# Attention scores from zero-padded states, fewer split operands, and a planner that keeps GpSimd and VectorE apart

## The chip, the core and the metric

The program runs on one core of one Trainium2 chip. The metric is the device time of one execution in microseconds (us). TensorE is called PE here (PEld is its weight load, which overlaps the matmuls), VectorE is DVE, ScalarE is ACT, GpSimd is POOL, and SyncE (SP) issues every DMA of this kernel. TensorE has two clock levels, 1.2 and 2.4 GHz; the profile gives the granted share of the higher one (PEclk: 1.00 is 2.4 GHz).

## What is computed

The reference, cut to what matters. Batch 8, 8 heads, 512 positions, 32 states, head size 64; the two feed-forward layers have 4608 tokens, width 512 and inner width 1536.

```python
def _attn_ref(x, state):                      # x (8,8,512,64), state (8,8,32,64)
    scores = scale * x @ state^T              # softmax over the 32 states  -> xread = a @ state
    scores2 = scale * state @ x^T             # softmax over the 512 tokens -> sread = a2 @ x
    return concatenate([xread, sread], axis=2)

x = attention output as rows of 512           # 8 * (512 + 32) = 4608 tokens
x = ((x @ w_a) * (x @ w_b)) @ w_out           # first layer
x = (silu(x @ w_gate) * (x @ w_val)) @ w_out  # second layer
```

Only the last array is returned.

## The kernel before, in words

**Numbers.** Most products are computed as sums of products of split operands: `hi_lo` (lines 319 to 328) makes `hi`, a rounded copy that PE takes at one pass (`R32`), on ACT (line 324), and `lo = x - hi` on DVE or POOL (`subtract`, line 317). A product then takes three matmuls (hi·hi, hi·lo, lo·hi). A matmul on unsplit `F32` operands needs no preparation but costs PE more. Weights come as 64-bit floats; `convert` (lines 339 to 379) turns each into 32-bit ones with two ACT, three or so DVE and one POOL instruction, the last of which (line 375, an integer add) only POOL may do.

**Stages.** The batches are called blocks 0 to 7, and `s` is the block of all state rows. About the first 760 us compute attention and the first layer: attention block by block, the products of states and weights (`state_w`, lines 431 and 432), the first layer's two products (`gemm`, line 645) and its output product (`out_part`, line 680). In the shadow of that the second layer's weights are converted, combined and written back to DRAM (`second_weights`, line 700 on). From about 760 us on the second layer runs over four pairs of blocks: at the start of a pair `operands` forms sums of its inputs (line 738) and splits them, then `second` runs products pA to pD (line 750), combinations (764, 771) and output products (`unit`, line 844; partial sums at 862).

**Attention.** `attention` runs once a block and `quad` twice (a quad is two pairs of heads, j = 0 and 1, each of 64 score rows). `quad` loads two `xt` tiles, makes scores `sT` (128 rows, 512 tokens), and calls `softmax1` (lines 520 to 553: DVE transposes and reductions, result split for the first layer) and `softmax2` (lines 555 on: result `sread`). There are two ways through it, chosen by `split`, which is true for blocks from `FROM_SPLIT` = 2 on:

- unsplit (blocks 0, 1): for each j one F32 matmul of 64 weight columns into its own half of the PSUM rows (line 511), one copy to `sT`; in `softmax2` one copy of the turned weights `pa` to `a2`, and four F32 matmuls with `xn` (line 605).
- split (blocks 2 to 7): `xt` is split; the states' tile `stt` has hi in one half of its 128 columns and lo in the other (lines 471 to 474), so that two matmuls a j give both halves (line 494), which ACT copies across (line 500) and DVE adds (line 503); in `softmax2` `pa` is split into `a2`, `xn` (1024 columns) into `xnh` and `xnl`, and twelve matmuls follow.

**Order.** Nothing is issued as it is written. Every instruction is a task of `Program` with buffers, dependencies, a due time `by`, and for some a `start`; `order` is a list scheduler that plays the whole program through with the costs at lines 62 to 67 and gives each engine's queue an order. A task that ACT, DVE or POOL may do goes to the engine that comes free, unless another is planned to finish it earlier. At run time each engine takes its queue strictly in that order. All DMAs are on SP's queue. PSUM banks, and the shared buffer classes `w` (44) and `h` (20), are counted in the plan.

Of the kernel before, what the change touches and what calls it, by code (L numbers as in the profile page):

```python
# [44 lines left out]
FROM_SPLIT = 2  # L45
# [18 lines left out]
HOP_US, PE_HOP_US = 0.15, 0.3  # L64
DMA_US, DMA_ISSUE_US, DMA_BYTES_PER_US = 2.2, 0.5, 3.6e5

# [3 lines left out]
def act(n):  # L70
    return {"ACT": ACT_US[0] + ACT_US[1] * n}
# [11 lines left out]
class Buf:  # L83


    def __init__(self, tag, name, make, after=None):
        self.tag, self.name, self.make, self.after = tag, name, make, after
        self.t = None
        self.parts = {}
        self.tasks = set()  # L90
# [10 lines left out]


class Program:
# [8 lines left out]
    def add(self, engines, fn, r=(), w=(), by=1e9, start=0.0, size=0):  # L112
# [24 lines left out]
        self.tasks.append(t)  # L137
        return t

    def order(self):  # L140
# [16 lines left out]
        wire = 0.0  # L157
        events = []
# [9 lines left out]
        while events:  # L168
# [18 lines left out]
            for e, heap in ready.items():  # L187
                if free[e] > now + 1e-9:
                    continue
                held = []  # L190
                while heap:
# [21 lines left out]
                    free[e] = end = now + us  # L213
                    main = max(main, t.main)
# [27 lines left out]
class Kernel:  # L242
# [32 lines left out]
    def bank(self, name, out=None):  # L275

        if out is not None:
            return self.ring(f"po{out}", 1, name, self.ps)
        return Buf("pt", name, lambda: self.ps.tile([P, 512], F32, tag="pt", bufs=ROOM["pt"], name=name))
# [4 lines left out]
    def ring(self, tag, n, name, pool=None, dtype=F32, shape=(512,)):  # L284
# [6 lines left out]
        )  # L291
        old.append(b)
# [162 lines left out]
    def attention(self, b, start, span, split, by_x, by_s):  # L455


        nc, p = self.nc, self.p
        raw_st = self.load(
            self.h_buf(f"strt{b}"), self.st_t[b], P * 1024, lambda t: t[:, :256], start=start  # L460
        )
        st = lambda: raw_st.t[:, :256].rearrange("p (j n) -> p j n", n=64)
        tt = None
        if split:
            tt = self.w_buf(f"stt{b}", R32, (NPAIR, P))
            for par in range(2):
                o = 64 * par
                hi = lambda par=par, o=o: tt.t[:, par::2, o:o + 64]
                lo = lambda par=par, o=o: tt.t[:, par::2, 64 - o:128 - o]
                src = lambda par=par: st()[:, par::2]  # L470
                self.p.add(act(128), lambda e, hi=hi, src=src: nc.scalar.copy(hi(), src()), [raw_st], [(tt, (par, 0))])
                self.subtract(
                    lo, src, lambda hi=hi: hi().bitcast(F32), dve_pool(128), [raw_st, (tt, (par, 0))], [(tt, (par, 1))]
                )
        return [
            self.quad(b, g, start + span * g / 2, span, raw_st, st, tt, by_x, by_s) for g in range(2)
        ]

    def quad(self, b, g, t0, span, raw_st, st, tt, by_x, by_s):

        nc, p = self.nc, self.p
        split = tt is not None
# [3 lines left out]
        if split:  # L486
            tmp = self.h_buf(f"tmp{nm}")
            for j in range(2):
                s = self.split(f"xts{nm}_{j}", x[j])
                ps = self.bank(f"psc{nm}_{j}")  # L490

                def fn(pe, j=j, s=s, ps=ps):
# [3 lines left out]
                self.pe(2 * PASS_US, fn, [tt, s], [ps], by=t0 + span * 0.15)  # L496
                own, oth = slice(64 * j, 64 * j + 64), slice(64 - 64 * j, 128 - 64 * j)
                kw = {"by": t0 + span * 0.15 + 2}
                p.add(
                    act(512), lambda e, own=own, oth=oth, ps=ps: nc.scalar.copy(tmp.t[own], ps.t[oth]),  # L500
                    [ps], [(tmp, j)], **kw
                )
                self.vec(512, lambda v, own=own, ps=ps: v.tensor_tensor(
                    out=sT.t[own], in0=ps.t[own], in1=tmp.t[own], op=ALU.add
                ), [ps, (tmp, j)], [(sT, j)], **kw)
        else:
            ps = self.bank(f"psc{nm}", g if b == 0 else None)

            def fn(pe, ps=ps):
                for j in range(2):  # L510
                    pe.matmul(
                        ps.t[64 * j:64 * j + 64], lhsT=st()[:, 2 * g + j], rhs=x[j].t, start=True, stop=True
                    )

            self.pe(8 * PASS_US, fn, [raw_st, x[0], x[1]], [ps], by=t0 + span * 0.15)
            self.copy(lambda: sT.t, lambda ps=ps: ps.t, 512, [ps], [sT], by=t0 + span * 0.15 + 2)
        x_hl = self.softmax1(b, g, sT, by_x)
        self.softmax2(b, g, sT, split, by_s)
        return x_hl

    def softmax1(self, b, g, sT, by):
# [7 lines left out]
        self.vec(512, lambda v: v.transpose(sn.t, sT.t), [sT], [sn], **kw)  # L529
        self.vec(  # L530
            512, lambda v: v.tensor_reduce(mx.t[:, :, 0], grouped(sn.t), axis=AX.X, op=ALU.max), [sn], [mx], **kw
# [8 lines left out]
            512, lambda v: v.tensor_reduce(sm.t[:, :, 0], grouped(sn.t), axis=AX.X, op=ALU.add), [sn], [sm], **kw  # L540
# [11 lines left out]
        self.vec(512, lambda v: v.transpose(at.t, sn.t), [sn], [at], **kw)  # L552
        return self.split(f"xs{nm}", at, **kw)

    def softmax2(self, b, g, sT, split, by):
# [11 lines left out]
        self.vec(620, first, [sT], [st], start=by - 35, **kw)  # L567
# [17 lines left out]
        if split:  # L585
            a2 = self.split(f"a2{nm}", pa, psum=True, **kw)
            xh, xl = self.w_buf(f"xnh{nm}", R32, (1024,)), self.w_buf(f"xnl{nm}", R32, (1024,))
            self.hi_lo(xn, lambda: xn.t, xh, lambda: xh.t, xl, lambda: xl.t, 1024, **kw)
            parts = [xh, xl]
        else:  # L590
            a2 = self.h_buf(f"a2{nm}")
            self.copy(lambda: a2.t, lambda: pa.t, 512, [pa], [a2], **kw)
            parts = [xn]
        ps = self.bank(f"psr{nm}")

        def fn(pe):
            terms = []
            for c in range(4):
                l, r = slice(c * P, (c + 1) * P), slice(c * 256, (c + 1) * 256)
                if split:  # L600
                    terms += [(a2.t[:, ha, l], parts[hx].t[:, r]) for ha, hx in ((0, 0), (0, 1), (1, 0))]
                else:
                    terms.append((a2.t[:, l], xn.t[:, r]))
            for n, (l, r) in enumerate(terms):
                pe.matmul(ps.t[:, :256], lhsT=l, rhs=r, start=n == 0, stop=n == len(terms) - 1)

        self.pe(1.32 if split else 1.75, fn, [a2, *parts], [ps], **kw)
# [398 lines left out]
def laid_out(inputs):  # L1006
# [6 lines left out]
    st_t = np.zeros((B, 2, D, NPAIR, 2, NS), state.dtype)  # L1013
    for h in range(2):
        st_t[:, h, :, :, h] = sp[:, :, h].transpose(0, 3, 1, 2)
    arrays["st_t"] = st_t.reshape(B, P, NPAIR * 2 * NS)
# [32 lines left out]
```

## Time and profile before

| | us |
|---|---|
| median of 3 runs | 1563.6 (1561.76 to 1568.19) |
| the profiled execution | 1562.1 |
| its span, first to last instruction | 1560.3 |
| PE busy | 1482.2 (95%) |
| DVE busy | 1109.7 (71%) |
| ACT busy | 675.9 (43%) |
| POOL busy | 360.3 (23%) |
| mean granted clock of PE | 0.985 |

Matmuls overlap in the pipeline, so the busy time of PE is the time in which at least one is under way; what PE takes for a matmul is read from the start of one to the start of the next. An engine's busy time includes time in which an instruction is under way but held up.

### The profile page before, as it was taken

The numbers are of one execution on the slowest core, as the hardware profiler recorded it, in microseconds if no ns is written. First come the engines' busy times: TensorE is split into PE (matmuls) and PEld (weight loads), VectorE is DVE, ScalarE is ACT, GpSimd is POOL, SyncE is SP. The second block draws the span as 40 slices with busy tenths as digits, with TensorE's granted clock in tenths as the row PEclk, the third lists the DMA queues.
The fourth block names the chain that finished last, engine by engine and source line by source line (L and its number), as shares of the span: only waits on it lengthen the run. The fifth ranks groups of instructions, "written<-read, shape, count | busy, mean of one in ns | idle before, by whom it ended". The sixth has DMA issues, their size and how long they took to land.

```text
span 1560.3 us, 19362 instructions
## 1 busy us (share of the span) xinstructions
PE 1482.2 (95%) x6792; PEld 1218.3 (78%) x6792; DVE 1109.7 (71%) x1676; ACT 675.9 (43%) x1196; POOL 360.3 (23%) x256
## 2 busy tenths in 40 slices
PE   4798899899999999999999989999999999999998
PEld 1577687688887888898777778888788887888887
DVE  8999767866789898776686896555855568545554
ACT  6676655653556576554442432221413123222220
POOL 3525212421234343333321340000200021000000
PEclk9899999899999999999999999999999999999999
DMA  7665564563455555656875668646464555622411
GB/s 285 211 236 197 177 220 145 176 205 122 152 189 206 202 205 216 230 203 216 334 259 200 238 236 305 220 157 221 167 231 168 189 202 173 218 95 108 162 68 68
DMA packets 111185, 304.84 MB, mean 195 GB/s; under 512 B 11760, under 2 KB 13808, under 8 KB 111088
## 3 DMA queue, kind: packets, MB, share of 16 engines
q1 hardware_dynamic: 111088, 303.61, 54.8%
q8 instruction: 53, 0.87, 0.2%
q14 instruction: 44, 0.36, 0.1%
HBM read 222.30 MB, written 80.74 MB: 194 GB/s over the span
## 4 chain that ended last, share of the span: by engine, by line
PE 52%; DVE 8%; issue 2%; DMA 1%; ACT 1%; POOL 1%; SPq 0%; DVEq 0%; POOLq 0%; ACTq 0%
PE pu L844 15%; PE pC L750 7%; PE pB L750 7%; PE pA L750 7%; PE pD L750 3%; PE po L680 3%; PE p L645 3%; PE p_s L645 2%; DVE s L738 1%; PE pvs L645 1%; PE pgs L645 1%; PE pus L844 1%; DVE x L317 1%; PE po_s L680 1%; DVE t L764 1%
## 5 line engine op out<-in xcount | busy, mean ns | idle before, releaser
L680 PE MATMUL po<-hs,wo 128*128 128x512 f32 x1152 | 289.7, 395 | 2.6 <-ACT hs L324 1.5
L645 PE MATMUL p<-xs,swh 128*128 128x512 f32 x768 | 243.4, 398 | 15.0 <-ACT xs L324 5.5
L680 PEld LDWEIGHTS po<-hs,wo 128*128 128x128 f32 x1152 | 218.3, 191 | 48.6 <-ACT hs L324 1.9
L645 PEld LDWEIGHTS p<-xs,swh 128*128 128x128 f32 x768 | 144.7, 191 | 50.2 <-DVE a L664 6.5
L645 PE MATMUL p<-xs,swl 128*128 128x512 f32 x384 | 151.8, 395 | 1.2 <-DVE swl L317 1.1
L750 PE MATMUL pB<-x,w 128*128 128x512 f32 x576 | 146.6, 390 | 2.0 <-DVE t L764 2.0
L750 PE MATMUL pA<-x,wg 128*128 128x512 f32 x576 | 148.0, 393 | 0.0
L844 PE MATMUL pu<-wo,hv 128*128 128x512 f32 x576 | 140.6, 389 | 0.0
L844 PE MATMUL pu<-wo,hu 128*128 128x512 f32 x576 | 138.6, 389 | 0.0
L750 PEld LDWEIGHTS pB<-x,w 128*128 128x128 f32 x576 | 108.2, 188 | 25.4 <-DVE t L764 2.8
L750 PEld LDWEIGHTS pA<-x,wg 128*128 128x128 f32 x576 | 109.5, 190 | 23.1
L844 PEld LDWEIGHTS pu<-wo,hu 128*128 128x128 f32 x576 | 107.9, 188 | 22.2
L844 PEld LDWEIGHTS pu<-wo,hv 128*128 128x128 f32 x576 | 107.9, 188 | 22.2
L768 ACT ACTIVATE av<-t 128x512 f32<-128x512 f32 x48 | 30.4, 632 | 211.2 <-DVE t L764 211.1
L317 POOL TENSOR_TENSOR hv<-av,hv 128x512 fp32r<-128x512 f32 x21 | 33.8, 1610 | 379.9 <-ACT hv L324 346.6
L764 DVE TENSOR_TENSOR t<-c,pB 128x512 f32<-128x512 f32 x96 | 65.6, 683 | 72.0 <-PE pB L750 71.7
L317 POOL TENSOR_TENSOR hs<-a,hs 128x512 fp32r<-128x512 f32 x40 | 62.5, 1562 | 179.1 <-ACT hs L324 169.6
L664 DVE TENSOR_TENSOR a<-a,p 128x512 f32<-128x512 f32 x96 | 65.5, 682 | 50.4 <-PE p L645 48.5
L324 ACT CAST hs<-a 128x512 fp32r<-128x512 f32 x96 | 59.6, 621 | 69.3 <-DVE a L664 56.2
L645 PEld LDWEIGHTS p<-xs,swl 128*128 128x128 f32 x384 | 73.3, 191 | 17.6 <-DVE swl L317 2.0
L750 PE MATMUL pC<-x,wv 128*128 128x512 f32 x288 | 75.3, 398 | 9.9 <-DVE c L764 9.9
L862 DVE TENSOR_TENSOR part<-part,pu 128x512 f32<-128x512 f32 x64 | 43.8, 684 | 51.1 <-PE pu L844 51.1
(205 smaller groups left out, 2682.1 us busy)
## 6 DMA issues: line engine op xcount, KB each, us to landing
w<-w SPq DMA_DIRECT2D x120, 512.0 KB, 5.3
sw<-swo SPq DMA_DIRECT2D x96, 256.0 KB, 2.5
wg<-w2g SPq DMA_DIRECT2D x48, 512.0 KB, 4.7
wv<-w2v SPq DMA_DIRECT2D x48, 512.0 KB, 5.0
wo<-w2o SPq DMA_DIRECT2D x48, 512.0 KB, 5.6
swr<-sw SPq DMA_DIRECT2D x47, 512.0 KB, 5.1
raw_w<-in_wab SPq DMA_DIRECT2D x24, 512.0 KB, 6.5
xt<-in_xt SPq DMA_DIRECT2D x32, 256.0 KB, 5.5
```

The lines of the kernel that those rows point to most:

```text
L317: lambda e: self.by_engine[e].tensor_tensor(out=out(), in0=in0(), in1=in1(), op=ALU.subtract), r, w, **kw
L324: self.p.add(act(n), lambda e: self.nc.scalar.copy(hi(), src()), [src_buf], [hb], **kw)
L645: pe.matmul(ps.t[:, :n], lhsT=l, rhs=r, start=i == 0, stop=i == last)
L664: self.vec(n, lambda v, a=a, pb=pb: v.tensor_tensor(out=a.t[:, :n], in0=a.t[:, :n], in1=pb.t[:, :n], op=ALU.mult), [pb], [a])
L680: pe.matmul(ps.t[:, :n], lhsT=wo[f].t[:, hw, c], rhs=hs.t[:, hh, :n], start=st, stop=sp)
L738: self.vec(512, lambda e, o=o, a=a, b=b, op=op: e.tensor_tensor(out=o.t, in0=a.t, in1=b.t, op=op), [a, b], [o])
L750: pe.matmul(ps.t, lhsT=w.t[:, hw, c], rhs=x.t[:, hx], start=start and i == n == 0, stop=stop and i == 1 and n == 2, skip_group_check=True)
L764: self.vec(512, lambda e: e.tensor_tensor(out=out.t, in0=ta(), in1=tb(), op=op), [a, b], [out])
L768: p.add(act(n), lambda e: nc.scalar.activation(out=a.t[:, :n], in_=g.t[:, :n], func=AF.Sigmoid), [g], [a])
L844: pe.matmul(ps.t, lhsT=h.t[:, hh, c], rhs=wo[f].t[:, hw], start=f == steps[0] and i == 0, stop=f == steps[-1] and i == 2)
L862: self.vec(w, lambda v: v.tensor_tensor(out=to(), in0=part.t[:, j % 2, :w], in1=ps.t[:, :w], op=ALU.add), [ps, (part, j)], [ok], by=by)
```

## The change

`FROM_SPLIT` becomes 4: blocks 2 and 3 take the unsplit way for the scores. The states come zero-padded from the host: for each pair j the tile has 128 columns, of which the other j's 64 are zero, so all matmuls of a quad add into one PSUM bank of 128 rows. A split quad takes six matmuls (three terms for each j) and one copy; an unsplit one takes two full-width F32 matmuls. In `softmax2` nothing is split any more, in any block. The planner's part: a task that has no PSUM buffer is marked `port` (in `Program.add`), apart from DVE's transposes and reductions, which are marked not; a variable `shared` holds until when POOL or a port task of DVE is planned to run, and while it lies ahead POOL takes nothing and DVE takes only tasks without the mark. POOL takes a task that DVE could do too only while DVE has at least 0.9 us of unmarked work ready (`BESIDE_US`). The planned delay between engines, `HOP_US`, goes from 0.15 to 0.25.

```diff
-FROM_SPLIT = 2
+FROM_SPLIT = 4
-HOP_US, PE_HOP_US = 0.15, 0.3
+HOP_US, PE_HOP_US = 0.25, 0.3
+BESIDE_US = 0.9
@@ Program.add
+        t.port = not any(b.psum for b in t.bufs) if port is None else port
@@ Program.order
+        shared = 0.0
+                blocked = shared > now + 1e-9 and e in ("DVE", "POOL")
+                    if blocked and (e == "POOL" or t.port):
+                        held.append(item)
+                        continue
+                    if e == "POOL" and "DVE" in t.engines and sum(
+                        q[2].engines["DVE"] for q in ready["DVE"] if q[2].engine is None and not q[2].port
+                    ) < BESIDE_US:
+                        held.append(item)
+                        continue
+                    if e == "POOL" or e == "DVE" and t.port:
+                        shared = end
@@ attention
-        raw_st = self.load(
-            self.h_buf(f"strt{b}"), self.st_t[b], P * 1024, lambda t: t[:, :256], start=start
-        )
+        raw_st = self.load(self.h_buf(f"strt{b}"), self.st_t[b], start=start)
+        tt = self.split(f"stt{b}", raw_st) if split else None
@@ quad, split (before)
-                s = self.split(f"xts{nm}_{j}", x[j])
-                ps = self.bank(f"psc{nm}_{j}")
-                    for h in range(2):
-                        pe.matmul(ps.t, lhsT=tt.t[:, 2 * g + j], rhs=s.t[:, h], start=h == 0, stop=h == 1)
-                    act(512), lambda e, own=own, oth=oth, ps=ps: nc.scalar.copy(tmp.t[own], ps.t[oth]),
-                self.vec(512, lambda v, own=own, ps=ps: v.tensor_tensor(
-                    out=sT.t[own], in0=ps.t[own], in1=tmp.t[own], op=ALU.add
@@ quad, unsplit (before)
-                    pe.matmul(
-                        ps.t[64 * j:64 * j + 64], lhsT=st()[:, 2 * g + j], rhs=x[j].t, start=True, stop=True
-                    )
@@ quad (after)
+        if tt is not None:
+            xs = [self.split(f"xts{nm}_{j}", x[j]) for j in range(2)]
+            terms = lambda: [
+                (tt.t[:, hs, cols[j]], xs[j].t[:, hx]) for j in range(2) for hs, hx in ((0, 0), (0, 1), (1, 0))
+            ]
+        else:
+            xs = x
+            terms = lambda: [(raw_st.t[:, cols[j]], x[j].t) for j in range(2)]
+        def fn(pe):
+            pairs = terms()
+            for n, (l, r) in enumerate(pairs):
+                pe.matmul(ps.t, lhsT=l, rhs=r, start=n == 0, stop=n == len(pairs) - 1)
+        self.pe((8 if tt is None else 6) * PASS_US, fn, [tt or raw_st, *xs], [ps], by=t0 + span * 0.15)
+        self.copy(lambda: sT.t, lambda: ps.t, 512, [ps], [sT], by=t0 + span * 0.15 + 2)
@@ softmax2
-            a2 = self.split(f"a2{nm}", pa, psum=True, **kw)
-            self.hi_lo(xn, lambda: xn.t, xh, lambda: xh.t, xl, lambda: xl.t, 1024, **kw)
+        a2 = self.h_buf(f"a2{nm}")
+        self.copy(lambda: a2.t, lambda: pa.t, 512, [pa], [a2], **kw)
+                pe.matmul(ps.t[:, :256], lhsT=a2.t[:, l], rhs=xn.t[:, r], start=c == 0, stop=c == 3)
@@ laid_out
-    st_t = np.zeros((B, 2, D, NPAIR, 2, NS), state.dtype)
+    st_t = np.zeros((B, 2, D, NPAIR, 2, 2, NS), state.dtype)
```

The states' tile that is loaded for each block thus grows from 128 to 256 KB.

## Rows read from the trace of the kernel before

**Rows 1.** Busy us (and instructions) by stage: PE, PEld, DVE, ACT, POOL; clock, DMA.
```profile
0.00:60.00 60.00, 31.76 (x72) 15.16 (x72) 52.05 (x75) 38.29 (x64) 25.92 (x25) 0.97 0.72 260
60.00:200.00 140.00, 126.69 (x539) 100.58 (x538) 126.24 (x204) 102.65 (x191) 52.09 (x39) 0.97 0.60 209
200.00:310.00 110.00, 102.44 (x457) 82.01 (x456) 82.11 (x125) 61.92 (x110) 30.37 (x21) 0.95 0.50 169
310.00:700.00 390.00, 380.23 (x1920) 323.28 (x1921) 306.80 (x476) 225.24 (x403) 131.11 (x89) 0.99 0.55 193
700.00:950.00 250.00, 238.28 (x1023) 194.12 (x1022) 189.18 (x270) 102.42 (x174) 67.52 (x45) 0.97 0.69 253
950.00:1300.00 350.00, 347.20 (x1530) 286.57 (x1529) 215.22 (x315) 89.33 (x152) 37.24 (x23) 1.00 0.55 197
1300.00:1560.00 260.00, 255.56 (x1261) 216.60 (x1259) 138.05 (x216) 56.00 (x107) 16.07 (x15) 1.00 0.38 131
```

**Rows 2.** Waits of PE from 60 to 310 us: total, times, longest.
```profile
PE p L645 <- ACT xs L324: 5.5, 1, 5.5
PE sw L431 <- DVE a L311: 4.3, 1, 4.3
```

**Rows 3.** Waits of PE from 310 to 1000 us: total, times, longest.
```profile
PE pC L750 <- DVE c L764: 6.9, 3, 4.5
```

**Rows 4.** A DVE reduction: duration in ns, minimum, median, maximum.
```profile
L531 DVE TENSOR_REDUCE mx<-sn x16: 628/678/686, 9.2 to 610.8; 128x16 f32<-128x512 f32 x16
```

**Rows 5.** One of DVE's subtractions at L317, the same columns.
```profile
L317 DVE TENSOR_TENSOR xts<-xt,xts x16: 678/692/1785, 68.0 to 599.1; 128x512 fp32r<-128x512 f32 x16
```

**Rows 6.** Timeline of DVE around 560 us: start, us, instruction.
```profile
558.25 3.45 DVE L317 TENSOR_TENSOR xnl<-xn,xnh 128x1024 fp32r<-128x1024 f32 x2
561.62 1.78 DVE L317 TENSOR_TENSOR xts<-xt,xts 128x512 fp32r<-128x512 f32 x1
```

**Rows 7.** Timeline of POOL in the same stretch.
```profile
560.58 2.28 POOL L317 TENSOR_TENSOR xts<-xt,xts 128x512 fp32r<-128x512 f32 x1
```

**Rows 8.** DVE's operand sums at L738, durations as in rows 4.
```profile
L738 DVE TENSOR_TENSOR s<-s,x2l x8: 679/1479/1776, 748.7 to 1285.2; 128x512 f32<-128x512 f32 x8
```

**Rows 9.** Chain that ended last: start, us, what; two split quads, twelve passes.
```profile
571.79 2.87 PE psr L605 x24
576.50 2.72 PE p L645 x12
```

**Rows 10.** Timeline of PE: two unsplit quads of L605 and what follows.
```profile
136.45 3.72 PE L605 MATMUL psr<-xn,a 128*128 128x256 f32 x16 [0.65 <-ACT a L309]
139.82 0.58 PE L680 MATMUL po<-hs,wo 128*128 128x512 f32 x1
```

**Rows 11.** Timeline of PE: unsplit scores of two quads, then the first layer's first product.
```profile
13.63 2.55 PE L511 MATMUL psc<-xt,strt 128*64 128x512 f32 x4 [3.01 <-DMA xt<-in_xt]
...
40.05 1.98 PE L511 MATMUL psc<-xt,strt 128*64 128x512 f32 x4
41.96 1.22 PE L645 MATMUL p<-xs,swh 128*128 128x512 f32 x2
42.98 0.63 PE L645 MATMUL p<-xs,swl 128*128 128x512 f32 x1
```

**Rows 12.** Groups by shape: count, busy us, mean ns, idle before.
```profile
L503 DVE TENSOR_TENSOR sT<-psc,tmp 64x512 f32<-64x512 f32 x24 | 16.5, 687 | 1.5 <-ACT tmp L500 1.2
...
L317 DVE TENSOR_TENSOR xnl<-xn,xnh 128x1024 fp32r<-128x1024 f32 x11 | 15.9, 1448 | 0.7 <-ACT xnh L324 0.5
...
L500 ACT COPY tmp<-psc 64x512 f32<-64x512 f32 x24 | 14.0, 582 | 3.1 <-PE psc L494 2.5
...
L317 DVE TENSOR_TENSOR a<-pa,a 128x512 fp32r<-128x512 f32 x12 | 7.7, 682 | 2.4 <-ACT a L324 2.4
```

**Rows 13.** POOL's integer add of the conversions, durations as in rows 4.
```profile
L375 POOL TENSOR_TENSOR cv_w<-cv_w x24: 1282/1601/2274, 11.4 to 284.4; 128x512 int32<-128x512 int32 x24
```

**Rows 14.** Timeline of DVE in the start: one run of subtractions.
```profile
22.79 3.81 DVE L317 TENSOR_TENSOR w<-cv_w,w 64x512 fp32r<-64x512 f32 x5
```

More of the change, by code (lines that the diff above doesn't have):

```diff
@@ L88, in __init__ @@
         self.t = None
+        self.psum = False
         self.parts = {}
@@ L100, in __init__ @@
         self.engine, self.main = None, 0.0
+        self.port = False
 class Program:
@@ L110, in __init__, with add @@
         self.first = 0.0
-    def add(self, engines, fn, r=(), w=(), by=1e9, start=0.0, size=0):
+    def add(self, engines, fn, r=(), w=(), by=1e9, start=0.0, size=0, port=None):
         deps, bufs = set(), []
@@ L278, in bank @@
             return self.ring(f"po{out}", 1, name, self.ps)
-        return Buf("pt", name, lambda: self.ps.tile([P, 512], F32, tag="pt", bufs=ROOM["pt"], name=name))
+        b = Buf("pt", name, lambda: self.ps.tile([P, 512], F32, tag="pt", bufs=ROOM["pt"], name=name))
+        b.psum = True
+        return b
     def dram(self, name, shape, dtype=F32):
@@ L291, in ring @@
         )
+        b.psum = pool is self.ps
         old.append(b)
@@ L458, in attention, with quad @@
         nc, p = self.nc, self.p
-        raw_st = self.load(
-            self.h_buf(f"strt{b}"), self.st_t[b], P * 1024, lambda t: t[:, :256], start=start
-        )
[L462 to L473, printed above, removed]
-                )
+        raw_st = self.load(self.h_buf(f"strt{b}"), self.st_t[b], start=start)
+        tt = self.split(f"stt{b}", raw_st) if split else None
         return [
-            self.quad(b, g, start + span * g / 2, span, raw_st, st, tt, by_x, by_s) for g in range(2)
+            self.quad(b, g, start + span * g / 2, span, raw_st, tt, by_x, by_s) for g in range(2)
         ]
-    def quad(self, b, g, t0, span, raw_st, st, tt, by_x, by_s):
-        nc, p = self.nc, self.p
-        split = tt is not None
+    def quad(self, b, g, t0, span, raw_st, tt, by_x, by_s):
         nm = f"{b}_{g}"
@@ new lines, in quad @@
+        ps = self.bank(f"psc{nm}", g if b == 0 else None)
+        cols = [slice((2 * g + j) * P, (2 * g + j + 1) * P) for j in range(2)]
+        if tt is not None:
[3 more added lines that the diff above has]
+            ]
+        else:
+            xs = x
+            terms = lambda: [(raw_st.t[:, cols[j]], x[j].t) for j in range(2)]
@@ L517, in quad @@
+        def fn(pe):
[4 more added lines that the diff above has]
+        self.copy(lambda: sT.t, lambda: ps.t, 512, [ps], [sT], by=t0 + span * 0.15 + 2)
         x_hl = self.softmax1(b, g, sT, by_x)
-        self.softmax2(b, g, sT, split, by_s)
+        self.softmax2(b, g, sT, by_s)
@@ L528, in softmax1 @@
         kw = {"by": by}
-        self.vec(512, lambda v: v.transpose(sn.t, sT.t), [sT], [sn], **kw)
+        self.vec(512, lambda v: v.transpose(sn.t, sT.t), [sT], [sn], port=False, **kw)
         self.vec(
-            512, lambda v: v.tensor_reduce(mx.t[:, :, 0], grouped(sn.t), axis=AX.X, op=ALU.max), [sn], [mx], **kw
+            512, lambda v: v.tensor_reduce(mx.t[:, :, 0], grouped(sn.t), axis=AX.X, op=ALU.max), [sn], [mx], port=False, **kw
         )
@@ L539, in softmax1 @@
         self.vec(
-            512, lambda v: v.tensor_reduce(sm.t[:, :, 0], grouped(sn.t), axis=AX.X, op=ALU.add), [sn], [sm], **kw
+            512, lambda v: v.tensor_reduce(sm.t[:, :, 0], grouped(sn.t), axis=AX.X, op=ALU.add), [sn], [sm], port=False, **kw
         )
@@ L551, in softmax1, with softmax2 @@
         at = self.h_buf(f"at{nm}")
-        self.vec(512, lambda v: v.transpose(at.t, sn.t), [sn], [at], **kw)
+        self.vec(512, lambda v: v.transpose(at.t, sn.t), [sn], [at], port=False, **kw)
         return self.split(f"xs{nm}", at, **kw)
-    def softmax2(self, b, g, sT, split, by):
+    def softmax2(self, b, g, sT, by):
         nc = self.nc
@@ L565, in first @@
             v.tensor_scalar(out=st.t[:, 1:2], in0=st.t[:, 0:1], scalar1=-SCALE, scalar2=None, op0=ALU.mult)
-        self.vec(620, first, [sT], [st], start=by - 35, **kw)
+        self.vec(620, first, [sT], [st], start=by - 35, port=False, **kw)
         self.p.add(act(512), lambda e: nc.scalar.activation(
@@ L584, in softmax2 @@
         xn = self.load(self.w_buf(f"xn{nm}", F32, (1024,)), self.xn[b, g], P * 4096, start=by - 25)
-        if split:
-            a2 = self.split(f"a2{nm}", pa, psum=True, **kw)
-            xh, xl = self.w_buf(f"xnh{nm}", R32, (1024,)), self.w_buf(f"xnl{nm}", R32, (1024,))
-            self.hi_lo(xn, lambda: xn.t, xh, lambda: xh.t, xl, lambda: xl.t, 1024, **kw)
[L589 to L593, printed above, removed]
+        a2 = self.h_buf(f"a2{nm}")
+        self.copy(lambda: a2.t, lambda: pa.t, 512, [pa], [a2], **kw)
         ps = self.bank(f"psr{nm}")
         def fn(pe):
-            terms = []
             for c in range(4):
                 l, r = slice(c * P, (c + 1) * P), slice(c * 256, (c + 1) * 256)
[L600 to L607, printed above, removed]
+                pe.matmul(ps.t[:, :256], lhsT=a2.t[:, l], rhs=xn.t[:, r], start=c == 0, stop=c == 3)
+        self.pe(1.75, fn, [a2, xn], [ps], **kw)
         sr = self.h_buf(f"sr{nm}")
@@ L1012, in laid_out @@
     sp = state.reshape(B, NPAIR, 2, NS, D)
-    st_t = np.zeros((B, 2, D, NPAIR, 2, NS), state.dtype)
+    st_t = np.zeros((B, 2, D, NPAIR, 2, 2, NS), state.dtype)
     for h in range(2):
-        st_t[:, h, :, :, h] = sp[:, :, h].transpose(0, 3, 1, 2)
-    arrays["st_t"] = st_t.reshape(B, P, NPAIR * 2 * NS)
+        for j in range(2):
+            st_t[:, h, :, j::2, j, h] = sp[:, j::2, h].transpose(0, 3, 1, 2)
+    arrays["st_t"] = st_t.reshape(B, P, NPAIR * 4 * NS)
     st_1 = np.zeros((2, 2, D, H, NS, 4), state.dtype)
```

17 lines of the change are left out of this document (removed).

## The prediction

> **What bounds the kernel now.** I read the busy times by stage first, then what PE waited for, then the durations of DVE's and POOL's instructions against each other.
>
> The stages [rows 1] show that PE's stream sets the time nearly everywhere: from 950 to 1300 us PE is busy for 347.2 of 350 us. Time is lost where PE idles: 28.2 us before 60 us, 13.3 from 60 to 200, 7.6 from 200 to 310, 9.8 from 310 to 700, 11.7 from 700 to 950, 2.8 from 950 to 1300, and 4.4 at the end, where the last outputs drain. The granted clock falls in the same stages: one less the clock, times the length, is 4.2 us for 60 to 200, 5.5, 3.9 and 7.5 for the next three. So from 60 to 1300 us 45 us are idle and about 21 more were run at the lower clock level after an idle spell: 66 us is the most that a better order could return there.
>
> DVE is why PE idles. Idle share and DVE load go together [rows 1]: DVE 90% busy and PE idle 9.5% (60 to 200), 79% and 2.5% (310 to 700), 61% and 0.8% (950 to 1300). The waits name DVE's late results, or ACT's that follow them [rows 2, 3].
>
> Part of DVE's load is no work. A reduction, with one input, is 678 ns in the median and never over 686 [rows 4]; a subtraction, with two inputs in SBUF, is 692 in the median and reaches 1785 [rows 5]. Around 561 us both sides are to be seen: DVE's `xts` takes 1.78 us while POOL runs another for 2.28 us [rows 6, 7]. The two engines take turns at such operations, and the one that comes second is shown as busy. At the switch between pairs in the second layer half of one kind of sums are held up so (median 1479 against a minimum of 679 ns) [rows 8], and PE waits for their products.
>
> **The change part by part.**
>
> *PE: longer.* A 512-column pass is 2.72/12 = 0.227 us [rows 9]. Scores of a split quad go from four passes to six: 0.453 us, times 8 quads (blocks 4 to 7), 3.6 us. In `softmax2` two split quads took 2.87 us [rows 9], two unsplit 139.82 - 136.45 = 3.37 [rows 10]: 0.25 us a quad, times 12, 3.0 us. Blocks 2 and 3 replace four passes (0.91 us) by two full-width F32 matmuls of 512 columns. No row has one at full clock. From below: the F32 matmul of 256 columns is 3.37/8 = 0.42 us, so twice that for 512, 1.69 a quad. From above: the pair of half-width ones took 1.91 us at the lower clock level [rows 11] (that it was the lower one is seen from the two passes behind, 1.02 us), the two side by side; one after the other at full clock that is again 1.91. I take 1.69, which comes from full clock and full width: 0.78 times 4 quads, 3.1 us (4.0 at most). Sum: 9.7 us (10.6). All this lies in stages where PE is the bound and counts in full.
>
> Blocks 0 and 1 lose the side-by-side pair: 1.9 us more a quad at the lower level. Three of these four quads run by 16.2 us, where PE idles for its inputs anyway, but the fourth stands directly ahead of the first product at 41.96 us [rows 11]. Cost 1.9 us, between 0 (if it is ordered earlier) and 3.8 (if DVE's first input, too, is late by 1.9). The pair in one row, both done in 1.91 us, is the trace's side of this [rows 11]. The Trainium skill, "TensorEngine Tiling (Array Packing)", section Performance Considerations, has the rule, and it speaks against this part: weights of at most 64 columns can run as two column tiles at once. By it half-width matmuls would keep blocks 2 and 3 at 0.84 us a quad in place of 1.69, and the sum below would be 4 x 0.85 + 1.9 = 5.3 us lower; the padding gives that up, so the sum stays with the rows.
>
> *DVE and ACT: shorter.* Gone are the 24 half-height sums (687 ns, 16.5 us of DVE), the 24 copies across (14.0 us of ACT), 12 subtractions from PSUM (7.7 us of DVE) and the split of `xn` (11 subtractions of 1.22 to 1.45 us on DVE, one on POOL, and 12 casts on ACT) [rows 12]; 8 of the `xts` subtractions, 0.69 us in the median [rows 5]. Added are 12 copies of `sT` on ACT or DVE, 0.6 to 0.7 us each, and slightly longer splits of the states. DVE loses some 40 us, net of half the copies.
>
> *The planner: POOL's share.* POOL has 257 instructions [rows 1]; 72 are the integer adds of the conversions, which stay. Some 180 could go to DVE. A moved one costs DVE 0.69 us; one left on POOL holds up DVE's neighbour by up to 1.78 - 0.69 = 1.09 us [rows 5, 6]. So moving is about even for DVE's load, and I count it as 0. What is gained is order: a held-up instruction on DVE holds all that is queued behind it, PSUM copies for PE among them, and the plan now lets those pass first. In turn a marked task that is ready waits, in the plan, for POOL's instruction to end; behind it on its queue nothing stands, since the plan issues others first.
>
> *What comes back.* I read it from the relation between DVE load and PE idle above.
> - 60 to 200 us: 8 sums (5.5 us) and 8 `xts` (5.5 us) fall out, 2 copies come in: 126.2 becomes about 117 of 140, 83%. Between 79% (2.5%) and 90% (9.5%) that is 5.0% idle, 7.0 us in place of 13.3: 6.3 us, and half of the 4.2 us of clock: 8.4.
> - 200 to 310: of the removed work only the second softmax of blocks 2 and 3 lies here, 4 subtractions from PSUM and 4 of `xn`, some 7 of 82 us. I count a quarter of the 13.1 us (idle and clock) for it and the order: 3.3.
> - 310 to 700: DVE falls by some 20 of 307 us to 74%; between 61% and 79% that is 2.0% idle, 2 us less, with 1 us of clock: 3.
> - 700 to 950: no work goes, only hold-ups at the switches [rows 3, 8]: a third of 19.2 us: 6.4.
> - 950 to 1300: the switches again: 1.
> - Up to 60 us: the 5.5 us wait for `xs` at its end [rows 2] follows a DVE stretch with hold-ups; I take 2 us back.
> Together 24 us.
>
> The new delay between engines and the larger states' tile I cost at nothing: the first shifts due times of all tasks alike, the second adds 128 KB a block, below 0.5 us at 260 GB/s [rows 1], ahead of the scores; if the cover of other loads is gone it costs that once, at the start.
>
> Sum against the profiled execution, 1562.1 us: + 9.7 + 1.9 - 24 = 1549.7. This execution is 1.5 us below the median of the runs, 0.1%; I state 1549.
>
> **The rivals.**
>
> *A: nothing gained in order.* PE's waits could be chains of latency rather than load: results that pass PE, DVE, ACT and PE again, as in [rows 3]. Then only the removed work helps (8.4 + 3) and pays for the added passes: 1562.1 + 11.6 - 11.4 = 1562. For it: in the switches DVE's work does not shrink. It is also what comes out if the change does not do what it says: the plan's POOL subtraction is 0.2 + 2.6 x 0.512 = 1.53 us, DVE's 0.61, while POOL's add of that size is 1.28 at its shortest and DVE's 0.69 in the median [rows 5, 13], so engines that are apart in the plan may meet on the chip.
>
> *B: slower, because POOL starves.* In the plan POOL may start only when DVE is on an unmarked task or idle. The runs of marked subtractions are long: 3.81 us in the start without a break [rows 14]. The integer adds, 24 of them on the way from the first layer's weights to its products [rows 13], would stand behind such runs. This decides from the point where the weights of a feature pair come later than PE asks for them; PE is there already at the edge. If 8 of the 24 come 2 us late in PE's stream, that is 16 us, with as much clock again lost as idle before (a third, 5 us): with half of A's return, 1562.1 + 11.6 - 6 + 21 = 1589. Against it: the transposes, reductions and PSUM copies of four quads, unmarked, stand in the same stretch ([rows 4] has one kind), and beside each POOL may start.
>
> *C: much more.* If the exclusion was the cause of most idle time, three quarters of the 66 us come back, and 5 in the start: 1562.1 + 11.6 - 50 - 5 = 1519. I let the case begin where 37 us come back: 1537. Against it: the waits of PE are many short ones at different lines, not one [rows 2, 3].
>
> **How the numbers follow.** A measurement of this kernel can tell about 0.5%, 7.8 us. The forecast (1537 to 1556) 0.47; C (under 1537) 0.13; A (1556 to 1571) 0.21; B (over 1571) 0.19. Faster by over 0.5%: 0.60; within: 0.21; slower: 0.19. The range takes the forecast and A whole, the upper half of C and the lower end of B: 1526 to 1574.
>
> **What would show it.** Right: PE idle from 60 to 200 us near 7 us; the maxima of two-input DVE subtractions rarer than now and L738's median near 0.68; POOL's count well below 257; PE's own stream longer by some 10 us, scores at 1.36 us and 1.7 us a quad. Wrong: POOL's integer adds with long idle before them and PE waiting for `w` or `swl` (B); the same waits at the switches with unstretched sums (A); full-width F32 scores above 1.9 us a quad at full clock.

## The result

The changed kernel takes 1514.5 us (median of 4 runs, 1514.41 to 1515.76) where the kernel before, run beside it, took 1563.0: a ratio of 0.9685, with a 95% interval from 0.9668 to 0.9701. That is 48 us, against the 13 that were forecast, and below the stated range; it is the time of case C, to which the prediction gave 0.13. The ratios here and below leave out three executions that were far slower than the others of their kernel (7449 us of att_only, 1647 of plan4, 5557 of the kernel before).

The page of the profile after, its first part (span; busy time, share and count of each engine):

```profile
span 1512.8 us, 19096 instructions
...
PE 1471.7 (97%) x6760; PEld 1213.7 (80%) x6760; DVE 1069.6 (71%) x1792; ACT 649.5 (43%) x1148; POOL 111.9 (7%) x84
```

DVE's share is the same as before, 71%. POOL went from 256 instructions to 84: the 72 integer adds and twelve others. The same stages as in [rows 1], with the same columns:

```profile
0.00:60.00 60.00, 33.44 (x74) 15.96 (x74) 49.68 (x81) 35.63 (x58) 14.32 (x16) 0.78 0.78 282
60.00:200.00 140.00, 132.44 (x559) 103.08 (x560) 121.92 (x208) 98.39 (x181) 28.11 (x19) 0.98 0.60 214
200.00:310.00 110.00, 107.53 (x479) 86.91 (x479) 82.14 (x137) 68.66 (x121) 19.49 (x13) 1.00 0.56 194
310.00:700.00 390.00, 390.00 (x1952) 332.86 (x1951) 286.72 (x518) 213.96 (x384) 34.61 (x25) 1.00 0.56 196
700.00:950.00 250.00, 250.00 (x1105) 207.07 (x1104) 194.23 (x319) 97.27 (x164) 15.35 (x11) 1.00 0.76 281
950.00:1300.00 350.00, 350.00 (x1568) 290.89 (x1567) 226.67 (x355) 92.47 (x160) 0.00 (x0) 1.00 0.53 192
```

From 310 us on PE does not idle at all, and its clock does not fall. PE's waits after (total, times, longest), first from 60 to 310 us, then all from 310 us to the end:

```profile
PE p L624 <- DVE swl L338: 8.8, 1, 8.8
PE sw L452 <- ACT swo L330: 3.8, 6, 1.5
PE sw L452 <- DVE w L338: 2.6, 2, 2.2
...
PE sw L452 <- ACT swo L330: 0.2, 1, 0.2
```

The waits of [rows 3], and all of their kind, are gone. To compare kernels I take from each trace the time from the start of one matmul to the start of the next, less the median of that kind of matmul (names and shape), and sum it: this is what idle time and the lower clock cost together. The rest of the span is PE's own stream. For two kinds the median will not do, because many or all of their matmuls run in the start, between waits or at the lower clock: the unsplit F32 scores and the products of states and weights. They are charged at what they take at full clock: an unsplit quad, four records in the trace, 1.72 us full width and 1.12 side by side (see the price of the attention's part), a product's pass 0.227. Kernels with the same PE work then have the same stream within 1 us. In us, by stage:

| | 0 to 100 | 100 to 310 | 310 to 700 | 700 to 950 | 950 on | sum | own stream |
|---|---|---|---|---|---|---|---|
| before | 45.0 | 29.4 | 15.1 | 19.6 | 3.6 | 112.8 | 1447.5 |
| after | 44.7 | 8.9 | 0.0 | -0.3 | -0.5 | 52.7 | 1460.0 |

So 60 us of lost time came back, all of it after 100 us; the stream is 12.5 us longer, and the first 100 us lose what they lost before.

### The profile page after: what moved, and what is told of

It reads as the page before. It is cut to its first block, busy times and chain, and to the rows that moved or that the text cites. A ratio compares the mean times of both kernels' runs of the same rounds, so it can differ in the third digit from the quotient of the medians.

```text
span 1512.8 us, 19096 instructions
## 1 busy us (share of the span) xinstructions
PE 1471.7 (97%) x6760; PEld 1213.7 (80%) x6760; DVE 1069.6 (71%) x1792; ACT 649.5 (43%) x1148; POOL 111.9 (7%) x84
## 4 chain that ended last, share of the span: by engine, by line
PE 80%; DVE 1%; DMA 0%; issue 0%; ACT 0%; SPq 0%; DVEq 0%; ACTq 0%
PE pu L823 17%; PE po L659 12%; PE p L624 11%; PE pC L729 9%; PE pB L729 9%; PE pA L729 9%; PE pD L729 4%; PE p_s L624 2%; PE pvs L624 1%; PE po_s L659 1%; PE pgs L624 1%; PE pus L823 1%; PE psr L584 1%; PE psc L505 1%; DMA swr<-sw 0%; PE sw L452 0%
## 5 line engine op out<-in xcount | busy, mean ns | idle before, releaser
L659 PE MATMUL po<-hs,wo 128*128 128x512 f32 x1152 | 285.5, 392 | 0.0
L624 PE MATMUL p<-xs,swh 128*128 128x512 f32 x768 | 240.2, 394 | 1.0 <-DVE xs L338 0.5
L330 ACT COPY a<-p 128x512 f32<-128x512 f32 x81 | 47.5, 586 | 105.4 <-PE p L624 100.0
L338 DVE TENSOR_TENSOR hs<-a,hs 128x512 fp32r<-128x512 f32 x96 | 69.5, 725 | 14.0 <-ACT hs L345 13.3
```

The costliest lines, as they stand in the source:

```text
L330: self.nc.scalar.copy(out(), in_())
L338: lambda e: self.by_engine[e].tensor_tensor(out=out(), in0=in0(), in1=in1(), op=ALU.subtract), r, w, **kw
L624: pe.matmul(ps.t[:, :n], lhsT=l, rhs=r, start=i == 0, stop=i == last)
L659: pe.matmul(ps.t[:, :n], lhsT=wo[f].t[:, hw, c], rhs=hs.t[:, hh, :n], start=st, stop=sp)
```

## Experiments

Medians are of 4 or more runs; each ratio is to the kernel before, run beside it on the same chip, with its 95% interval. "Lost" is the sum defined above; "stretch" is DVE's time beyond the lower quartile of each kind of instruction, the time in which it is held up, both from the profiled execution.

| kernel | us | ratio | POOL count | stretch | lost | own stream |
|---|---|---|---|---|---|---|
| before | 1563 to 1564 | 1 | 256 | 124 | 112.8 | 1447.5 |
| after | 1514.5 | 0.9685 (0.9668 to 0.9701) | 84 | 30 | 52.7 | 1460.0 |
| att_only | 1560.6 | 0.998 (0.9969 to 0.9991) | 232 | 115 | 100.5 | 1460.5 |
| plan_only | 1515.8 | 0.970 (0.9685 to 0.9714) | 92 | 41 | 66.8 | 1447.2 |
| before_excl | 1519.4 | 0.9713 (0.9699 to 0.9728) | 201 | 73 | 71.8 | 1447.5 |
| before_nopool | 1522.9 | 0.975 (0.9731 to 0.9769) | 78 | 42 | 71.2 | 1447.4 |
| before_hop25 | 1541.0 | 0.9859 (0.9837 to 0.9881) | 256 | 119 | 92.1 | 1447.3 |
| before_costs | 1544.2 | 0.9869 (0.9853 to 0.9885) | 383 | 172 | 95.9 | 1448.0 |
| after_hop15 | 1520.3 | 0.9716 (0.9702 to 0.9731) | 83 | 41 | 59.5 | 1460.0 |
| after_beside0 | 1518.4 | 0.9717 (0.9701 to 0.9733) | 202 | 68 | 55.4 | 1460.1 |
| hop15_beside0 | 1514.6 | 0.9682 (0.9665 to 0.9698) | 197 | 61 | 52.7 | 1460.1 |
| after_noexcl | 1520.6 | 0.9717 (0.9702 to 0.9731) | 94 | 38 | 58.9 | 1460.1 |
| after_nopool | 1515.0 | 0.9688 (0.9667 to 0.9709) | 78 | 28 | 52.8 | 1460.0 |
| dummy_unknown | 1577.7 | 1.0085 (1.006 to 1.0111) | 269 | 166 | 120.8 | 1460.3 |
| dummy_known | 1555.0 | 0.9944 (0.9924 to 0.9964) | 268 | 153 | 91.5 | 1460.1 |
| after_side | 1512.7 | 0.9669 (0.9655 to 0.9683) | 84 | 32 | 54.6 | 1455.2 |
| plan4 | 1511.4 | 0.9657 (0.9641 to 0.9673) | 86 | 38 | 60.4 | 1449.3 |
| plan4_x | 1515.9 | 0.9689 (0.9673 to 0.9705) | 199 | 70 | 63.2 | 1449.9 |

### Which part of the change

**att_only** is the changed kernel with the old planner:

```diff
-HOP_US, PE_HOP_US = 0.25, 0.3
+HOP_US, PE_HOP_US = 0.15, 0.3
...
-                blocked = shared > now + 1e-9 and e in ("DVE", "POOL")
+                blocked = False
...
-                    if e == "POOL" and "DVE" in t.engines and sum(...) < BESIDE_US:
-                        held.append(item)
-                        continue
```

> The changed kernel with the planner of the kernel before (no exclusion, no condition on GpSimd, HOP_US 0.15): the attention's part alone. Theory P (the planner's part brings nearly all; the attention's part adds passes to PE and relieves an engine that is not the cause): 1545 to 1575 us. Rival W (the removed VectorE and ScalarE work brings most): 1520 to 1535 us. The prediction's own steps gave it 1562.

It took 1560.6 us. PE's stream grew by 13 us and 12 us of lost time came back: the attention's part pays for itself and no more. **plan_only** is the other half, the kernel before with the planner's lines of the diff and nothing of the attention's:

> The kernel before with the new planner alone (exclusion, the 0.9 us condition, HOP_US 0.25); attention as before. Theory P: 1505 to 1525 us, since PE's own stream is some 8 us shorter than in the changed kernel. Rival W: 1545 to 1560 us.

1515.8 us: the planner's part brings nearly everything. Theory P holds, rival W falls.

### Which part of the planner

**before_nopool** takes optional work off POOL and leaves the planner blind:

```diff
 def dve_pool(n):
-    return dve(n) | {"POOL": POOL_US[0] + POOL_US[1] * n}
+    return dve(n)
...
-        self.p.add(dve(512, True) | {"POOL": 1.9}, clamp, [], [hi], **kw)
+        self.p.add(dve(512, True), clamp, [], [hi], **kw)
```

> The kernel before, only that work which VectorE could do is never given to GpSimd (the integer adds of the conversions stay there); no other line of the planner changes. If what counts is that long GpSimd operations with collisions disappear, 1515 to 1535 us; if the planner has to know of the exclusion to order the rest, 1550 us or more; if VectorE lacks the room for that work, above 1563.

1522.9 us. DVE is busier than in the kernel before (1114.1 us against 1109.7), and PE loses 42 us less. So a plan that is blind to the exclusion does nearly as well when POOL is almost empty. **after_beside0** is the opposite: `BESIDE_US = 0.0`, so that POOL takes optional work again, with the exclusion in the plan.

> The changed kernel with the condition for GpSimd set to 0 us: the exclusion stays in the plan, and GpSimd takes optional work whenever the plan finds it earlier there. If the exclusion in the plan is what counts, 1513 to 1520 us, with more GpSimd instructions than 84 and few collisions; if it is the emptied GpSimd, 1530 us or more.

1518.4 us with 202 instructions on POOL: an emptied POOL is not needed either. Nor did the collisions become few, as was expected: DVE is held up for 68 us. Two more take single pieces out of the changed kernel, **after_hop15** (`HOP_US` 0.15) and **after_noexcl** (`blocked = False`, the rest kept):

> The changed kernel with the planned delay between engines back at 0.15 us. If the delay's gain (22 us in the kernel before) adds to that of the exclusion, 1530 to 1540 us; if both mend the same fault, a plan that is too early, 1512 to 1522 us.

> The changed kernel in which the plan never blocks on the exclusion; the 0.9 us condition and the 0.25 us delay stay. With GpSimd nearly empty by the condition, and little left to collide: 1514 to 1525 us; if the integer adds' collisions have to be planned, 1530 us or more.

1520.3 and 1520.6 us: each piece by itself can be missed at a cost of 6 us. **hop15_beside0** misses both the delay and the condition and keeps the exclusion alone, and **before_excl** does the same in the kernel before, with its own attention:

```diff
-HOP_US, PE_HOP_US = 0.25, 0.3
+HOP_US, PE_HOP_US = 0.15, 0.3
...
-BESIDE_US = 0.9
+BESIDE_US = 0.0
```

> The exclusion alone: the changed kernel with the delay at 0.15 us and the condition on GpSimd at 0 us, to be held against the attention's part alone (1560.6 us). If the plan's knowledge of the exclusion is enough by itself, 1515 to 1530 us; if it needs the emptied GpSimd or the longer delay, 1540 us or more.

> The kernel before, its attention and its 0.15 us delay unchanged, with the exclusion alone in the planner (no condition on GpSimd). If the exclusion by itself explains the gain, 1514 to 1525 us, with some 200 GpSimd instructions and stretched VectorE operations left; if the changed attention is needed for it, 1535 us or more.

1514.6 and 1519.4 us. The exclusion alone does it, in either attention: 45 us in the kernel before. Two-input DVE operations are still held up there. The operand sums of [rows 8], POOL's operand splits and PE's waits of [rows 3], all of before_excl (durations in ns, minimum, median, maximum; then waits from 310 us to the end):

```profile
L757 DVE TENSOR_TENSOR s<-s,x2l x8: 686/948/1629, 728.4 to 1245.6; 128x512 f32<-128x512 f32 x8
...
L336 POOL TENSOR_TENSOR x<-x2l,x x15: 1288/1572/1744, 725.8 to 1254.1; 128x512 fp32r<-128x512 f32 x15
L336 POOL TENSOR_TENSOR x<-s,x x13: 1284/1471/1751, 731.5 to 1265.6; 128x512 fp32r<-128x512 f32 x13
...
PE pC L769 <- DVE c L783: 0.4, 1, 0.4
```

POOL does 28 of these splits, 23 in the kernel before, and DVE's sums are stretched to 1629 ns, yet PE's wait for `c` is 0.4 us in all. What changed is what stands ahead of what. Here is DVE's queue at one switch of the kernel before, between 1104 and 1111 us, with PE's product that `t` waits for in the last line:

```profile
1105.29 0.68 DVE L317 TENSOR_TENSOR x<-x2l,x 128x512 fp32r<-128x512 f32 x1
1105.89 0.68 DVE L771 TENSOR_TENSOR au<-au,pA 128x512 f32<-128x512 f32 x1
1106.49 1.28 DVE L738 TENSOR_TENSOR s<-x2l,x2l 128x512 f32<-128x512 f32 x2
1107.69 0.68 DVE L738 TENSOR_TENSOR s<-x2l,s 128x512 f32<-128x512 f32 x1
1108.30 0.67 DVE L862 TENSOR_TENSOR part<-part,pu 128x512 f32<-128x512 f32 x1
1108.89 0.68 DVE L738 TENSOR_TENSOR s<-x2l,s 128x512 f32<-128x512 f32 x1
1109.50 0.67 DVE L764 TENSOR_TENSOR t<-c,pB 128x512 f32<-128x512 f32 x1
...
1105.19 1.52 PE L750 MATMUL pB<-x,w 128*128 128x512 f32 x6
```

And the same place in before_excl:

```profile
1067.19 1.77 DVE L336 TENSOR_TENSOR x<-x2l,x 128x512 fp32r<-128x512 f32 x1
1068.89 0.68 DVE L881 TENSOR_TENSOR part<-part,pu 128x512 f32<-128x512 f32 x1
1069.48 0.67 DVE L783 TENSOR_TENSOR t<-c,pB 128x512 f32<-128x512 f32 x1
...
1073.27 1.29 DVE L757 TENSOR_TENSOR s<-x2l,x2l 128x512 f32<-128x512 f32 x2
...
1067.54 1.52 PE L769 MATMUL pB<-x,w 128*128 128x512 f32 x6
```

In the kernel before four more sums `s` stand ahead of `t`, which starts 2.9 us after pB's last pass is done (1105.19 + 6 x 0.227 = 1106.55). The planner's own times can be had by playing `order` through again with its costs; the queues come out in the order of the trace. In that plan the sums just fit: `t` starts 0.4 us after pB's planned end (1022.06 and 1021.69 us). On the chip DVE falls 3.8 us further behind its plan between 1097.20 and 1105.29, in four operations that take 0.99 to 1.78 us where 0.61 was planned, and `t` pays for it. In before_excl those last four sums stand behind `t`, which follows pB by 0.6 us, though the split just before was held up (1.77 us). At the end the chip is 88 us behind the plan in the kernel before (planned 1472 us) and 30 us in before_excl (1489). Collisions that the order counts on cost little here.

### Is it the exclusion, or any plan that is less early?

**before_hop25** changes one number of the kernel before, the planned delay between engines. **before_costs** changes another line, so that the plan has the durations of the trace:

```diff
-ACT_US, DVE_US, FAST_US, POOL_US = ((0.09, 0.84e-3), (0.07, 1.05e-3), (0.07, 0.53e-3), (0.2, 2.6e-3))
+ACT_US, DVE_US, FAST_US, POOL_US = ((0.19, 0.84e-3), (0.15, 1.05e-3), (0.15, 0.53e-3), (0.2, 2.2e-3))
```

> The kernel before with the planned delay between engines at 0.25 instead of 0.15 us, nothing else. If the delay is a part of the gain, 1545 to 1555 us; if it only reorders, 1558 to 1568.

> The kernel before, planner without the exclusion, but with the durations that the trace shows: ACT 0.19 + 0.84 n, VectorE 0.15 + 1.05 n (fast ones 0.15 + 0.53 n), GpSimd 0.2 + 2.2 n (us, n in thousands of columns). If any plan that is less early mends the order, as the longer delay did, 1530 to 1548 us; if only the exclusion does, 1555 to 1568; a cheaper GpSimd in the plan also draws more work there, which makes it slower.

1541.0 and 1544.2 us: each brings some 20 us, with no knowledge of the exclusion. Their plans are hardly longer than that of the kernel before (1471 and 1475 us against 1472); what changes is the order. The second has more on POOL than any other kernel, and the most stretch of all (its page, first part):

```profile
PE 1476.5 (96%) x6792; PEld 1210.4 (78%) x6792; DVE 1098.3 (71%) x1578; ACT 660.1 (43%) x1167; POOL 527.4 (34%) x383
```

172 us of stretch against 124, and yet 17 us less lost time. So held-up DVE time as such is not what PE loses; what fits all of these kernels is that PE loses where the plan runs ahead of the chip. The exclusion is the largest part by which it ran ahead, not the only one. No run made the plan still earlier, and none changed the order at random; how far chance in the order alone moves the time is seen only from the kernels with the exclusion, which lie between 1511 and 1520 us (dummy_known apart).

### Putting the collisions back

The base is **after_nopool**, the changed kernel without optional work for POOL:

> The changed kernel in which GpSimd is never given work that VectorE could do (72 integer adds stay). It is the base of the two kernels with additional work. Expected 1514 to 1521 us under every theory: the changed kernel gives GpSimd only a handful of such operations anyway.

1515.0 us. Into it go 190 additional POOL operations, one beside about every second 512-column split: in **dummy_unknown** they are issued with DVE's own instruction and the planner does not know, in **dummy_known** they are tasks that it places. They do work whose result nobody uses.

```diff
 # dummy_unknown, in hi_lo
+        extra = n == 512 and not psum and self.count % 2
+        def fn(e):
+            if extra:
+                self.nc.gpsimd.tensor_tensor(
+                    out=self.spare.t, in0=src()[:, :500], in1=hi().bitcast(F32)[:, :500], op=ALU.subtract
+                )
+            self.by_engine[e].tensor_tensor(out=lo(), in0=src(), in1=hi().bitcast(F32), op=ALU.subtract)
...
 # dummy_known, in hi_lo
+            self.p.add({"POOL": POOL_US[0] + POOL_US[1] * n}, lambda e: self.nc.gpsimd.tensor_tensor(
+                out=self.spare.t, in0=src()[:, :500], in1=hi().bitcast(F32)[:, :500], op=ALU.subtract
+            ), [src_buf, hb], [(self.spare, self.count)], **kw).beside = beside
```

> The base, and beside every second of VectorE's 512-column splits GpSimd does the same subtraction once more (500 columns) into a spare tile that nobody reads; the planner is not told of it. Theory U (the kernel before lost its time to collisions that its fixed order had not planned): 1535 to 1565 us, with PE idle after 100 us again. Rival L (what costs is VectorE's load, stretched operations included, and there is room for that now): 1514 to 1525 us.

> The base with the same additional GpSimd operations, but as tasks of their own that the planner places by its exclusion rule, with the due time of the split beside them. Theory U: 1514 to 1530 us, clearly below the kernel in which the planner does not know of them. Rival L: both kernels the same, within 5 us.

1577.7 and 1555.0 us. The unknown operations bring the whole loss back and more, 63 us (theory U had at most 50), and with it the wait of [rows 3] (longest wait of PE from 310 us on, first in dummy_unknown, then in dummy_known):

```profile
PE pC L737 <- DVE c L751: 13.1, 5, 4.7
...
PE pA L739 <- ACT c L334: 3.9, 3, 2.2
```

Not all of it need be DVE's hold-ups: the plan did not count on POOL's own time either, and the integer adds stand behind these operations. From 950 us on, where no adds run any more, 14 us are lost against none in after_nopool. Known to the plan the same operations cost 40 us, not the 0 to 15 that theory U expected: knowing is worth 23 us here, so theory U is borne out in part only. Of these 40 some 10 stand in the plan itself (its planned end is 1501 us, after_nopool's 1491); the rest arises on the chip, which drifts from the plan (153 us of stretch in spite of a plan without any). These operations come on top of DVE's work, where those of before_excl come in its place; whether that is the reason, no run shows.

### The price of the attention's part

**after_side** runs the unsplit scores as half-width pairs on the padded tile:

```diff
+            if tt is None:
+                for j in range(2):
+                    own = slice(64 * j, 64 * j + 64)
+                    pe.matmul(ps.t[own], lhsT=raw_st.t[:, cols[j]][:, own], rhs=x[j].t, start=True, stop=True)
+                return
```

> The changed kernel with the unsplit scores of blocks 0 to 3 as pairs of half-width matmuls side by side, on the same zero-padded tile. By the prediction's price of the padding, 0.85 us in each of 4 quads where PE is the bound, and up to 1.9 us in the start: 1509 to 1511 us. If the start is set by other things and only the four quads count, 1511 to 1512.

1512.7 us, 1.8 less than the changed kernel and above both expected ranges; its runs (1511.6 to 1514.4) reach up to the other's fastest (1514.41), so it is no more than a hint. The quads themselves can be read. PE's timeline at one of them, first after, then after_side:

```profile
97.39 1.88 PE L505 MATMUL psc<-xt,strt 128*128 128x512 f32 x4
98.70 1.03 PE L624 MATMUL p<-xs,swh 128*128 128x512 f32 x2
...
95.84 1.08 PE L506 MATMUL psc<-xt,strt 128*64 128x512 f32 x4
96.85 0.73 PE L629 MATMUL p<-xs,swh 128*128 128x512 f32 x2
```

Two such `p` take 0.62 us elsewhere, so the full-width quad holds up the stream for 98.70 - 97.39 + 1.03 - 0.62 = 1.72 us (forecast 1.69) and the side-by-side one for 1.12: 0.60 us a quad is the price of the padding, not 0.85. The two side by side are 1.5 times as fast as the padded pair, not twice.

**plan4** and **plan4_x** join what was learned: the attention of the kernel before with `FROM_SPLIT = 4`, whose unsplit way has the half-width pairs already, under the new planner, and under the exclusion alone.

> A version put together from the experiments: the whole new planner, the attention of the kernel before, and blocks 2 and 3 on its unsplit way (half-width scores side by side). PE's stream is shorter than the changed kernel's by 0.85 us in 4 quads, 0.45 in 8 and 0.25 in 8, some 9 us; if nothing else moves, 1506 to 1511 us; if VectorE's additional work (some 35 us) brings waits back, 1514 us or more.

> The same version with the exclusion alone (delay 0.15 us, no condition on GpSimd). If condition and delay are not needed, within 4 us of the version before it: 1505 to 1512 us; if VectorE needs its GpSimd help with the split attention, it is the faster of the two.

1511.4 and 1515.9 us: plan4 lies at the upper end of its first range, plan4_x above its own. plan4 has the lowest median of all, 3 us below the changed kernel, but in separate comparisons whose intervals overlap. Its stream is 11 us shorter (9 expected), and 8 us more are lost, 6 of them before 310 us. With the split attention the condition and the delay are together worth 4 us, with the changed attention nothing (hop15_beside0); why, no run shows.

## Why the prediction was wrong

- **PE's own stream: right.** 9.7 + 1.9 us were charged, and it is 12.5 us longer. Six passes for a split quad's scores take 1.36 us as forecast (320.78 to 322.14 us), the full-width F32 quad 1.72 for 1.69.

```profile
320.78 1.52 PE L505 MATMUL psc<-xts,stt 128*128 128x512 f32 x6
322.14 1.52 PE L659 MATMUL po<-hs,wo 128*128 128x512 f32 x6
```

- **What the attention's part returns: right in sum.** Case A priced removed work against added passes at 1562; the part alone measured 1560.6.
- **The fourth quad ahead of the first product: wrong in place.** It was ordered earlier (36.22 us), and the first product still starts at 41.95. But the start did not gain the 2 us that were taken: the 5.5 us wait for `xs` is gone, and a longer one stands in its place. DVE and POOL collide four times in a row, and PE waits 8.8 us for the `swl` behind them (timeline of DVE, then of POOL, after):

```profile
52.27 4.62 DVE L392 SCALAR_TENSOR_TENSOR cv_w<-raw_w,cv_w 128x512 uint32<-128x512 uint32 x4
56.81 1.48 DVE L389 TENSOR_SCALAR cv_wo<-cv_wo 128x512 uint32<-128x512 uint32 x1
58.22 2.28 DVE L338 TENSOR_TENSOR swl<-swr,swh 128x1024 fp32r<-128x1024 f32 x1
...
53.04 6.37 POOL L396 TENSOR_TENSOR cv_w<-cv_w 128x512 int32<-128x512 int32 x4 [22.54 <-DVE cv_w L392]
```

- **POOL's share, moving is even for DVE's load: right**, and it misled. In before_nopool 178 instructions move, and DVE is busy for 4.4 us more.
- **What comes back: the step that failed.** I read PE's idle share off DVE's load. That relation held between stages of one kernel and not between plans. From 310 to 700 us DVE's load fell as forecast, to 73.5% (74%), and PE's idle share went to 0, not to 2.0%; from 700 to 950 us DVE is busier than before (194.2 us against 189.2), and PE's 11.7 us of idle time are gone too. In the prediction's own measure (idle time, and one less the clock times the length, from [rows 1] and the rows after) these stages returned, in us:

| | 60 to 200 | 200 to 310 | 310 to 700 | 700 to 950 | 950 to 1300 | sum |
|---|---|---|---|---|---|---|
| forecast | 8.4 | 3.3 | 3 | 6.4 | 1 | 22.1 |
| measured | 7.1 | 10.6 | 13.7 | 19.2 | 2.8 | 53.4 |

So 60 to 200 us came out as forecast, the 3 us of the relation for 310 to 700 did not, nor did the quarter and the third that were taken for the order elsewhere without a row behind them. The prediction named the cause, a held-up instruction that holds the queue behind it, and then sized it as a fraction of the loss instead of asking which of PE's waits had any other cause: after 310 us it was all of it.

- **The signs of being right could not tell.** All of them came: 7.6 us of idle PE from 60 to 200 us, the sums of [rows 8] at 0.684 us in the median, POOL at 84, the scores as above. They hold in case C as well, so they did not separate the forecast from it. The sums, after:

```profile
L717 DVE TENSOR_TENSOR s<-s,x2l x8: 683/684/687, 723.1 to 1238.1; 128x512 f32<-128x512 f32 x8
```

- **Case C: the mechanism was right, and the reason given against it was not.** Many short waits at different lines fit a fault of the plan, since a plan that runs ahead is late wherever PE asks next. The 5 us that the case took for the start did not come.
- **Case B: its sign came, not its price.** PE's wait for `w` after 60 us is 2.6 us in all. But the adds above come bunched after POOL had idled for 22.5 us, with PE waiting for `swl` behind them, and in two pairs of kernels the exclusion makes the first 100 us worse: 44.7 us are lost in the changed kernel against 40.6 in after_noexcl, 51.3 in before_excl against 45.0 in the kernel before. In the third pair it does not (43.1 in hop15_beside0, 43.8 in att_only).
- **"The first shifts due times of all tasks alike": wrong.** The delay, costed at nothing, brings some 22 us by itself in the kernel before (before_hop25): in `order` it also sets from when a task counts as ready, and so the order. Under the exclusion, taking it back costs 6 us while the condition is kept (after_hop15); taking back both costs nothing with the changed attention (hop15_beside0) and 4 us with the split one (plan4_x).

What stays open: why dummy_known loses 40 us, and what sets the first 100 us, which no kernel here brought below 40 us of lost time.

## What to carry to other kernels

Where queues are ordered ahead of time by a model, ask first how far the model runs ahead of the chip, and put into it whatever makes engines wait for each other: one planned rule was worth 45 us where collisions were still allowed, and a more cautious delay alone half of that. Engine load says little about such losses; compare, at each wait of the bounding engine, what its supplier did just before and whether that had to come first. A step that is known as a cause but sized by a fraction should get a range that reaches from none to all of the loss.

## What the runs showed of the hardware

DVE and POOL take turns, instruction by instruction, at some of their operations: in the start after, DVE's run of four two-input operations takes 4.62 us (the first two 0.69 each, the last two, beside POOL's, 1.75) and four of POOL's 6.37 (1.28 alone at the shortest, [rows 13]). DVE's reductions are not held up [rows 4], nor its sums with an input in PSUM: the 96 at line 664 of the kernel before are never over 689 ns.

```profile
L664 DVE TENSOR_TENSOR a<-a,p x96: 629/682/689, 46.9 to 760.4; 128x512 f32<-128x512 f32 x96
L363 DVE TENSOR_SCALAR cv_o<-cv_o x12: 415/422/1309, 441.9 to 900.1; 128x512 f32<-128x512 f32 x12
```

The second row is one of DVE's fast operations on one SBUF input, 422 ns in the median where the first row's kind takes 682, and it is held up too. The Trainium skill, "GPSIMD Engine Reference", section 8, says that POOL shares its SBUF interfaces with DVE and that DVE instructions with two SBUF inputs or in a mode that uses both ports contend. The trace agrees: these two kinds are stretched, to 1785 [rows 5] and 1309 ns, and in the kernel before no transpose, reduction or operation with an input in PSUM is. That the fast operation runs in such a mode the trace does not say.
